# A memory-bound decode kernel: the last 512 columns of one wq row per partition, in place of 384, go to other partitions, spread over five DMA engines instead of three

## The chip, the cores and the metric

One core of a Trainium2 chip runs the kernel. The metric is device time in microseconds (us) of one launch; lower is better. In what follows PE is TensorE (the matrix multiplier), DVE VectorE, ACT ScalarE, and SP the engine whose queue issues the loads. The kernel before takes 138.09 us (median of 6 runs, 137.95 to 138.22).

## The reference

A decode step with four tokens: layer norm, attention over the last 2,048 positions of a cache, output projection, residual, then layer norm and a gated MLP with its residual. Every weight and cache row is read once, 55.6 MB in all.

```python
# shapes: x (4,1,1024); k_cache, v_cache (4,4,8192,128); wq (1024,4096); wo (4096,1024)
#         w1, w3 (1024,3584); w2 (3584,1024); all bf16
def A(x, k_cache, v_cache, wq, wo):        # 32 query heads, 4 kv heads, window W = 2048
    q = (x @ wq).reshape(...)              # <- the change touches how wq is loaded
    p = softmax(q . k[last W] / sqrt(128))
    return (p . v[last W]) @ wo
h   = x + A(layernorm(x), ...)
out = h + (silu(layernorm(h) @ w1) * (layernorm(h) @ w3)) @ w2
```

## The kernel before

All weights and caches flow through one ring (a buffer that is filled and freed in turn) in SBUF, the on-chip memory, by loads of 128 partitions issued from one queue, in the order wq, k, v, wo, w1, w3, w2. Partition p holds the eight wq rows 8p to 8p+7. The last 384 columns of each partition's eighth row do not go to the ring: the tail load stops short of them, and three small loads ("side" loads) put these 128 pieces of 768 B onto 12, 12 and 8 partitions.

```python
CE = 384
SETS = [(0, 3, 5), (60, 3, 5), (120, 2, 1)]      # first row, engines, pieces side by side per partition

def load_side(r0, ne, ns):
    t = ktpool.tile([P, JG * QD * 16], BF16, tag="kT")
    rows = A_wq[r0 * KC : (r0 + ne * 4 * ns) * KC, N_Q - CE : N_Q]
    rows = rows.rearrange("(t i k) n -> k i t n", i=ne, k=KC)[KC - 1]
    nc.sync.dma_start(out=t[: ne * 4, : ns * CE], in_=rows)
    return [t[: ne * 4, k * CE : (k + 1) * CE] for k in range(ns)]

def load_tail(at, src, n, r0, m):
    t = ring[:, at : at + m * n]
    nc.sync.dma_start(out=t[:, : m * n - CE], in_=src[:, r0 * n : (r0 + m) * n - CE])
    return [t[:, k * n : (k + 1) * n] for k in range(m)]

plan = [
    ("wq", load_rows, (0, wq_v, N_Q, 0, 4)),      # 4 rows a partition: 32,768 B each
    ("side", load_side, SETS[0]), ("side", load_side, SETS[1]), ("side", load_side, SETS[2]),
    ("wq", load_tail, (32 * KIB, wq_v, N_Q, 4, 4)),
    # ... k, v, wo, w1, w3 ...
    ("w2", load_rows, (56 * KIB, w2_v, D, 0, 17)),
    ("w2", load_rows, (90 * KIB, w2_v, D, 17, 7)),
    ("w2", load_rows, (104 * KIB, w2_v, D, 24, 3)),
    ("w2", load_rows, (110 * KIB, w2_v, D, 27, 1)),
]
# ...
x_sb = act.tile([B, D], BF16)
nc.scalar.dma_start(out=x_sb[:], in_=x_flat)     # 4 partitions: its packets mark engines 0 to 3
load_next(8)
# ... layer norm; xs / ts_ps / xsT hold the entries of x that belong to the side pieces ...
for kc in range(KC):
    # ... q += xnT[kc] @ wq[kc], the last 384 columns left out at kc == 7 ...
    if kc == RQ - 1:
        for k, np_ in enumerate(sl):             # the side pieces: 11 small matmuls
            nc.tensor.matmul(q_ps[QD * (JG - 1) : QD * (JG - 1) + B, CQ - CE : CQ],
                             lhsT=xsT[:np_, k, :], rhs=loaded["side"][k], start=False, stop=False)
```

Why anyone would do this: a 128-partition load is split over 16 DMA engines, eight partitions each. The side loads run on the lowest-numbered engines alone. The Trainium skill, "DMA: Bandwidth & Descriptors", section "Why a DMA increments its semaphore by 16 and not by 1" ("How many engines (k)"), says that a load runs on the largest k up to 16 that divides the slowest dimension of both sides, and on the lowest-numbered k of the engines. Here these are 12 partitions and 3 blocks of rows, so three engines, and the trace agrees: it has packets of 768 B in three engines' sequences alone, 44, 44 and 40 of them. So the piece takes 6,144 B from every engine and loads three of them with more: it moves work from engine to engine.

Of the kernel before, what the change touches and what calls it, by code (L numbers as in the profile page):

```python
# [14 lines left out]
BF16 = mybir.dt.bfloat16  # L15
# [4 lines left out]
def kernel(  # L20
# [13 lines left out]
    nc = tc.nc  # L34

    B, _, D = A_x.shape
# [5 lines left out]
    KC = D // P  # L42
# [16 lines left out]
    wide = ctx.enter_context(tc.tile_pool(name="wide", bufs=2))  # L59
    const = ctx.enter_context(tc.tile_pool(name="const", bufs=1))  # L60
    act = ctx.enter_context(tc.tile_pool(name="act", bufs=1))
# [46 lines left out]
    N_Q, N_F = Hq * Dh, F  # L108


    CE = 384
    SETS = [(0, 3, 5), (60, 3, 5), (120, 2, 1)]

    def load_side(r0, ne, ns):

# [11 lines that stand above are left out]
    KIB = 512  # L127
    plan = [
        ("wq", load_rows, (0, wq_v, N_Q, 0, 4)),
        ("side", load_side, SETS[0]),  # L130
        ("side", load_side, SETS[1]),
        ("side", load_side, SETS[2]),
        ("wq", load_tail, (32 * KIB, wq_v, N_Q, 4, 4)),
# [16 lines left out]
    def load_next(n=1):  # L150
        for _ in range(n):
            if cursor[0] < len(plan):
                kind, f, args = plan[cursor[0]]
                loaded.setdefault(kind, []).extend(f(*args))
                cursor[0] += 1
# [19 lines left out]
    for c in range(2):  # L175
# [8 lines left out]
        out=xn[:], in0=x_sb[:], scalar1=mv[:, 0:1], scalar2=rstd[:, 0:1],  # L184
# [9 lines left out]

    NS = sum(ns for _, _, ns in SETS)
    ts_ps = psA.tile([P, NS, B], BF16, tag="kt1")
    xs = wide.tile([B, NS, 12], BF16, tag="w4k")
    sl = []
    for r0, ne, ns in SETS:
        v = xn[:, r0 * KC : (r0 + ne * 4 * ns) * KC]  # L200
        v = v.rearrange("b (s l i k) -> b k l i s", s=4, l=ns, i=ne)
        nc.vector.tensor_copy(
            out=xs[:, len(sl) : len(sl) + ns, : ne * 4].rearrange("b l (i s) -> b l i s", s=4),
            in_=v[:, KC - 1, :, :, :],
        )
        for l in range(ns):
            nc.tensor.transpose(
                out=ts_ps[: ne * 4, len(sl), :], in_=xs[:, len(sl), : ne * 4], identity=ident[:B, :B]
            )
            sl.append(ne * 4)  # L210
    xsT = act.tile([12, NS, B], BF16)
    nc.vector.tensor_copy(out=xsT[:, : NS - 1, :], in_=ts_ps[:12, : NS - 1, :])
    nc.vector.tensor_copy(out=xsT[:8, NS - 1 :, :], in_=ts_ps[:8, NS - 1 :, :])


    q_ps = psA.tile([P, CQ], FP32, tag="scores")
# [9 lines left out]
        out=perm[:].rearrange("p (h dq) -> p h dq", dq=JG),  # L226
        in_=ident[:].rearrange("p (dq h) -> p h dq", dq=JG),
# [12 lines left out]
    for j in range(2, JG):  # L240
        nc.vector.tensor_tensor(
            out=same[:, 0, :], in0=same[:, 0, :], in1=ident[:, j * QD : (j + 1) * QD], op=ALU.add
# [6 lines left out]
    for kc in range(KC):  # L249
        wq_t = loaded["wq"][kc]  # L250
        for hf in range(CQ // 512):
            for g in range(JG):
                c0 = g * CQ + hf * 512
                n = min(512, N_Q - CE - c0) if kc == KC - 1 else 512
                nc.tensor.matmul(  # L255
                    q_ps[QD * g : QD * g + B, hf * 512 : hf * 512 + n],
                    lhsT=xnT[:, kc, :],
                    rhs=wq_t[:, c0 : c0 + n],
                    start=(kc == 0),
                    stop=(kc == KC - 1),  # L260
                )
        if kc == RQ - 1:
            load_next()
            for k, np_ in enumerate(sl):
                nc.tensor.matmul(
                    q_ps[QD * (JG - 1) : QD * (JG - 1) + B, CQ - CE : CQ],
                    lhsT=xsT[:np_, k, :],
                    rhs=loaded["side"][k],
                    start=False,
                    stop=False,  # L270
                )
# [4 lines left out]
    for r in range(REP):  # L276
        nc.tensor.transpose(out=qt_ps[:, r, :], in_=q_sb[:, r * Dh : (r + 1) * Dh], identity=ident[:])
    nc.vector.tensor_copy(
        out=qz[:, :, : Hkv * QD].rearrange("p b (g z) -> p b g z", g=Hkv)[:, :, :, :REP],
        in_=qt_ps[:].rearrange("p r (g x) -> p x g r", g=Hkv)[:, :B, :, :],  # L280
# [24 lines left out]
    for u, (b, n) in enumerate(units):  # L305
        k_v = loaded["k"][b]
        kT = ktpool.tile([P, NJ, P], BF16, tag="kT")
        for t in range(NJ // TB):
            kt_ps = psA.tile([P, TB, P], BF16, tag=f"kt{nt % 4}")
            for jj in range(TB):  # L310
                nc.tensor.transpose(  # L311
                    out=kt_ps[:, jj, :], in_=k_v[:, n * NJ + t * TB + jj, :], identity=ident[:]
# [21 lines left out]
        out=Pm[:], in_=scores_ps[:], func=ACT.Exp, bias=nmax[:], scale=1.0, accum_out=rsum[:]  # L334
# [6 lines left out]
    for c in range(NSB):  # L341
# [4 lines left out]
        for g in range(Hkv):  # L346
            if g % 2 == 0:
                nc.vector.tensor_scalar(  # L348
                    out=z[:, :, g, :], in0=pt_ps[:], scalar1=mask[:, g : g + 1], scalar2=None, op0=ALU.mult
# [10 lines left out]
        out=Dm[:], in0=ident[:].rearrange("p (g b r) -> p b g r", g=Hkv, b=B),  # L360
# [11 lines left out]
    for b in range(B):  # L372
        for j in range(JK):
# [5 lines left out]
                stop=(j == JK - 1),  # L379
# [19 lines left out]
    for i in range(IO):  # L399
        for j in range(JG):  # L400
# [5 lines left out]
                stop=(i == IO - 1),  # L406
# [27 lines left out]
        out=hn[:], in0=h1[:], scalar1=tot[:, 0:1], scalar2=rstd2[:, 0:1],  # L434
# [5 lines left out]
        out=hnT[:].rearrange("p k x -> p (k x)"), in_=hn[:].rearrange("q (c k) -> q k c", k=KC)  # L440
# [5 lines left out]
    def gate_up(kind, out_ps):  # L446
# [27 lines left out]
        out=hgT[:].rearrange("p i x -> p (i x)"),  # L474
        in_=hg[:].rearrange("q s c -> q (s c)").rearrange("q (c i) -> q i c", i=IF),
# [3 lines left out]
    for i in range(IF):  # L479
        for j in range(JG):  # L480
# [5 lines left out]
                stop=(i == IF - 1),  # L486
# [36 lines left out]
```

## Time and profile before

| | before |
|---|---|
| time, median of 6 runs | 138.09 us |
| span of the profiled run | 136.2 us |
| TensorE / VectorE / ScalarE busy | 52% / 32% / 23% |
| queue of the loads | 55.58 MB, 95.5% of 16 engines' span |
| last landing of a weight load | 132.80 us |

From the page of the kernel before: busy tenths of the DMA engines in 40 equal slices, then the queues (packets, MB, share of 16 engines' span).

```profile
DMA  5999999999999999999989999999899999999970
## 3 DMA queue, kind: packets, MB, share of 16 engines
q1 hardware_dynamic: 2728, 55.58, 95.5%
q8 instruction: 8, 0.13, 0.3%
q10 hardware_dynamic: 48, 0.02, 0.1%
q14 instruction: 2, 0.02, 0.0%
```

The DMA engines are 80% busy or more from the second slice to the 38th. The chain of waits says the same from the other end; its last pieces (start, length, what; a DMA piece runs from the issue of a load to its landing):

```profile
3.70 19.98 DMA ring<-in_A_wq_dram
...
73.34 1.46 PE OT_ps L374 x48
74.82 24.12 DMA ring<-in_B_w_dram
98.98 2.41 PE g_ps L451 x21
...
101.52 31.28 DMA ring<-in_B_w_dram
...
132.84 0.32 PE y_ps L481 x4
```

At 74.82 us the attention matmuls (OT_ps) have freed room in the ring, w1 is issued and lands 24.1 us later, behind the loads that were issued before it. The last load of w2 is issued at 101.5 us and lands after 31.3 us, at 132.80; PE and the store need little after that. These pieces are time in the queue, not slowness of one load: the engines never run dry. A kernel whose end is set by a stream of loads is bound by whichever of the 16 engines finishes last, because a load has landed only when all its engines have.

**Reading the engines one by one.** The profile's views add the engines up. The trace also has one record for each DMA packet, with start, duration, size and queue, but not its engine. On one engine a packet starts 3 to 4 ns before the one ahead of it is recorded as ended, and every engine must go through the same known sequence of sizes (eight packets a load, then a 4 B completion). Matching ends to starts under that rule gives 16 sequences with no packet left over. Engines that did the same work then agree within about 10 ns over 119 us, which is the check on the method. Its weak point: two engines whose packets end within a few ns of each other can be exchanged. Below, times in the stream count from the start of the first packet of the loads (1.73 us into the span), and the "finish" of an engine is the start of its last completion record.

What the sequences of the kernel before hold, apart from the same loads for all:

| engines | extra work | finish |
|---|---|---|
| 0, 1, 2 | 44, 44, 40 side pieces of 768 B, one every 33 ns | 130.62, 130.74 (order unknown), 130.49 |
| 3 | one 8 KB packet of queue 14 in between | 130.08 |
| eight others | one 16 KB packet of queue 8 ("instruction") each: "hit" below | 130.24 to 130.76 |
| four others | none | 128.83 to 129.35 |

An instruction packet takes 0.88 to 0.96 us, and the data packet after it takes 0.4 to 0.5 us longer than its like: 1.42 us in all for that engine. The first three rows are nearly level, and the four unhit engines are done 1.4 us early or more.

### The profile page before, as it was taken

What the parts mean: (1) busy time and instruction counts of PE and PEld (TensorE: products, weight loads), DVE (VectorE), ACT (ScalarE), POOL (GpSimd) and SP (SyncE); (2) the same over time, 40 slices, a digit from 0 to 9 for tenths busy, and PEclk for the clock granted to TensorE, in tenths of its full rate; (3) what the DMA queues carried; (4) which work ended last, traced back from release to release, by engine and by line L of the source; (5) the groups of instructions that cost most, each with busy time, mean ns of one, the idle gap of its engine ahead of it and who ended that gap; (6) DMA issues with size and microseconds to landing.
All of it is one profiled execution on the core that took longest, in us unless ns stands there. A gap on an engine that the chain in (4) does not pass through costs nothing.

```text
span 136.2 us, 2356 instructions
## 1 busy us (share of the span) xinstructions
PE 71.4 (52%) x1057; PEld 44.1 (32%) x1057; DVE 43.2 (32%) x78; ACT 31.0 (23%) x36; POOL 1.7 (1%) x8
## 2 busy tenths in 40 slices
PE   0202980969898989602275858810095440900960
PEld 0200220266565656200054747610042210300830
DVE  6810000054343425454972030260000794080000
ACT  3000000037373737445666000000004200000001
POOL 5000000000000000000000000000000000000000
PEclk9999999999999999955555595995559555555586
DMA  5999999999999999999989999999899999999970
GB/s 156 463 464 406 407 432 411 424 438 424 428 438 414 443 428 424 438 532 462 443 385 424 448 424 392 489 392 455 362 413 443 430 455 442 419 419 407 420 280 5
DMA packets 2786, 55.75 MB, mean 409 GB/s; under 512 B 308, under 2 KB 468, under 8 KB 728
## 3 DMA queue, kind: packets, MB, share of 16 engines
q1 hardware_dynamic: 2728, 55.58, 95.5%
q8 instruction: 8, 0.13, 0.3%
q10 hardware_dynamic: 48, 0.02, 0.1%
q14 instruction: 2, 0.02, 0.0%
HBM read 55.59 MB, written 0.01 MB: 408 GB/s over the span
## 4 chain that ended last, share of the span: by engine, by line
DMA 55%; PE 21%; ACT 13%; DVE 5%; SPq 2%; issue 1%; ACTq 0%
DMA ring<-in_B_w_dram 41%; DMA ring<-in_A_wq_dram 15%; PE kt_ps L311 9%; ACT kT L317 6%; PE scores_ps L296 5%; ACT z L352 3%; PE q_ps L255 3%; PE g_ps L451 2%; SPq L119 2%; DVE rmax L328 2%; ACT Pm L333 2%; PE OT_ps L374 2%; DVE pT L342 1%; DVE z L348 1%; ACT L333 1%
## 5 line engine op out<-in xcount | busy, mean ns | idle before, releaser
L317 ACT COPY kT<-kt_ps 128x1024 bf16<-128x1024 bf16 x16 | 15.8, 1013 | 12.0 <-PE kt_ps L311 12.0
L311 PE MATMUL kt_ps<-ident,ring 128*128 128x128 bf16 x256 | 16.5, 219 | 0.0
L311 PEld LDWEIGHTS <-ring 128*128 128x128 bf16 x256 | 14.4, 98 | 5.0 <-issue 4.9
L315 DVE COPY kT<-kt_ps 128x1024 bf16<-128x1024 bf16 x16 | 11.1, 692 | 15.2 <-PE kt_ps L311 15.2
L451 PEld LDWEIGHTS <-hnT 128*32 128x32 bf16 x128 | 5.2, 134 | 23.7 <-issue 21.0
L255 PE MATMUL q_ps<-ring,xnT 128*4 128x512 bf16 x64 | 7.2, 621 | 10.5 <-DMA ring<-in_A_wq_dram 10.5
L296 PE MATMUL scores_ps<-kT,qz 128*32 128x512 bf16 x64 | 9.9, 610 | 3.1 <-ACT kT L317 3.1
L451 PE MATMUL u_ps<-ring,hnT 128*32 128x448 bf16 x64 | 6.4, 576 | 8.7 <-DMA ring<-in_B_w_dram 8.7
L374 PE MATMUL OT_ps<-z,ring 128*128 128x32 bf16 x256 | 7.5, 186 | 5.7 <-ACT z L352 5.0
L451 PE MATMUL g_ps<-ring,hnT 128*32 128x448 bf16 x64 | 5.1, 496 | 9.5 <-DMA ring<-in_B_w_dram 9.5
L481 PE MATMUL y_ps<-ring,hgT 128*32 128x256 bf16 x112 | 5.6, 362 | 8.5 <-DMA ring<-in_B_w_dram 8.4
L374 PEld LDWEIGHTS <-ring 128*128 128x128 bf16 x256 | 7.3, 103 | 6.4 <-issue 6.4
L481 PEld LDWEIGHTS <-hgT 128*32 128x32 bf16 x112 | 4.3, 126 | 10.4 <-issue 6.2
L273 DVE TENSOR_SCALAR q_sb<-q_ps 128x512 bf16<-128x512 f32 x1 | 0.7, 692 | 19.9 <-PE q_ps L255 19.9
L255 PEld LDWEIGHTS <-xnT 128*4 128x4 bf16 x64 | 2.0, 116 | 14.6 <-issue 14.5
L491 ACT CAST res<-y_ps 128x256 bf16<-128x256 f32 x1 | 0.4, 372 | 26.8 <-PE y_ps L481 26.8
L352 ACT ACTIVATE z<-pt_ps,mask 128x512 bf16<-128x512 f32 x8 | 5.3, 688 | 3.5 <-DVE z L348 3.5
L401 PE MATMUL y_ps<-ring,o 128*32 128x256 bf16 x128 | 5.4, 344 | 1.3 <-DMA ring<-in_A_wo_dram 1.3
L274 ACT ACTIVATE q_sb<-q_ps 128x512 bf16<-128x512 f32 x1 | 0.6, 597 | 23.8 <-DVE q_sb L273 23.8
L344 PE MATMUL pt_ps<-pT,perm 128*128 128x512 bf16 x4 | 2.4, 609 | 6.8 <-DVE pT L342 6.8
L348 DVE TENSOR_SCALAR z<-pt_ps,mask 128x512 bf16<-128x512 f32 x8 | 5.5, 740 | 1.2 <-ACT z L352 0.8
L465 DVE RECIPROCAL eg<-eg 128x896 f32<-128x896 f32 x1 | 5.8, 5753 | 0.0
(80 smaller groups left out, 50.9 us busy)
## 6 DMA issues: line engine op xcount, KB each, us to landing
ring<-in_A_k_cache_dram SPq DMA_DIRECT2D x4, 2048.0 KB, 25.4
ring<-in_A_v_cache_dram SPq DMA_DIRECT2D x4, 2048.0 KB, 38.8
ring<-in_B_w_dram SPq DMA_DIRECT2D x1, 7168.0 KB
ring<-in_B_w_dram SPq DMA_DIRECT2D x2, 3584.0 KB, 27.9
ring<-in_B_w_dram SPq DMA_DIRECT2D x1, 4352.0 KB
ring<-in_A_wq_dram SPq DMA_DIRECT2D x1, 4096.0 KB, 12.1
ring<-in_A_wq_dram SPq DMA_DIRECT2D x1, 4000.0 KB, 20.0
ring<-in_B_w_dram SPq DMA_DIRECT2D x1, 1792.0 KB
```

The lines of the kernel that those rows point to most:

```text
L255: nc.tensor.matmul(q_ps[QD * g : QD * g + B, hf * 512 : hf * 512 + n], lhsT=xnT[:, kc, :], rhs=wq_t[:, c0 : c0 + n], start=(kc == 0), stop ...
L296: nc.tensor.matmul(scores_ps[QD * g : QD * (g + 1), n * 512 : (n + 1) * 512], lhsT=qz_v[:, z0 : z0 + QD], rhs=kT_v[:, g, :, :], start=(b = ...
L311: nc.tensor.transpose(out=kt_ps[:, jj, :], in_=k_v[:, n * NJ + t * TB + jj, :], identity=ident[:])
L315: nc.vector.tensor_copy(out=kT[:, t * TB : (t + 1) * TB, :], in_=kt_ps[:])
L317: nc.scalar.copy(out=kT[:, t * TB : (t + 1) * TB, :], in_=kt_ps[:])
L348: nc.vector.tensor_scalar(out=z[:, :, g, :], in0=pt_ps[:], scalar1=mask[:, g : g + 1], scalar2=None, op0=ALU.mult)
L352: nc.scalar.mul(out=z[:, :, g, :], in_=pt_ps[:], mul=mask[:, g : g + 1])
L374: nc.tensor.matmul(OT_ps[:, b, :], lhsT=loaded["v"][b][:, j, :], rhs=PTz[j // NJ][:, (j % NJ) * B + b, :, :], start=(j == 0), stop=(j == J ...
L401: nc.tensor.matmul(y_ps[QD * j : QD * (j + 1), :], lhsT=o4[:, i, :, :].rearrange("p b s -> p (b s)"), rhs=loaded["wo"][i][:, j * CG : (j + ...
L451: nc.tensor.matmul(out_ps[QD * j : QD * (j + 1), hf, :HF], lhsT=hnT[:, k, :], rhs=loaded[kind][k][:, c0 : c0 + HF], start=(k == 0), stop=( ...
L465: nc.vector.reciprocal(out=eg[:], in_=eg[:])
L481: nc.tensor.matmul(y2_ps[QD * j : QD * (j + 1), :], lhsT=hgT[:, i, :], rhs=loaded["w2"][i][:, j * CG : (j + 1) * CG], start=False, stop=(i ...
```

## The change

Its intent, as far as the code shows it: take more from every engine (512 columns, 8 x 1,024 B instead of 8 x 768 B) and, so that engines 0 to 2 do not get more than they have, let engines 3 and 4 take a part. 80 rows go to 20 partitions (20 and 5: five engines, 16 rows each), 48 rows in two loads to 12 partitions (three engines, 16 more rows each). The wq columns that are loaded this way now are a whole 512-column block of the matmul, so one of the 64 matmuls falls away.

```diff
@@ -108,8 +108,8 @@
     N_Q, N_F = Hq * Dh, F
 
 
-    CE = 384
-    SETS = [(0, 3, 5), (60, 3, 5), (120, 2, 1)]
+    CE = 512
+    SETS = [(0, 5, 4), (80, 3, 2), (104, 3, 2)]
 
     def load_side(r0, ne, ns):
 
@@ -194,7 +194,7 @@
 
     NS = sum(ns for _, _, ns in SETS)
     ts_ps = psA.tile([P, NS, B], BF16, tag="kt1")
-    xs = wide.tile([B, NS, 12], BF16, tag="w4k")
+    xs = wide.tile([B, NS, 20], BF16, tag="w4k")
     sl = []
     for r0, ne, ns in SETS:
         v = xn[:, r0 * KC : (r0 + ne * 4 * ns) * KC]
@@ -208,9 +208,11 @@
                 out=ts_ps[: ne * 4, len(sl), :], in_=xs[:, len(sl), : ne * 4], identity=ident[:B, :B]
             )
             sl.append(ne * 4)
-    xsT = act.tile([12, NS, B], BF16)
-    nc.vector.tensor_copy(out=xsT[:, : NS - 1, :], in_=ts_ps[:12, : NS - 1, :])
-    nc.vector.tensor_copy(out=xsT[:8, NS - 1 :, :], in_=ts_ps[:8, NS - 1 :, :])
+    xsT = act.tile([20, NS, B], BF16)
+    k0 = 0
+    for _, ne, ns in SETS:
+        nc.vector.tensor_copy(out=xsT[: ne * 4, k0 : k0 + ns, :], in_=ts_ps[: ne * 4, k0 : k0 + ns, :])
+        k0 += ns
 
 
     q_ps = psA.tile([P, CQ], FP32, tag="scores")
@@ -252,12 +254,14 @@
             for g in range(JG):
                 c0 = g * CQ + hf * 512
                 n = min(512, N_Q - CE - c0) if kc == KC - 1 else 512
+                if n <= 0:
+                    continue
                 nc.tensor.matmul(
                     q_ps[QD * g : QD * g + B, hf * 512 : hf * 512 + n],
                     lhsT=xnT[:, kc, :],
                     rhs=wq_t[:, c0 : c0 + n],
                     start=(kc == 0),
-                    stop=(kc == KC - 1),
+                    stop=(kc == KC - 1 or (kc == KC - 2 and c0 + 512 == N_Q)),
                 )
         if kc == RQ - 1:
             load_next()
```

## The prediction

> **What bounds the kernel.** The profile of before spans 136.2 us. Its DMA row is at 8 or 9 in all slices but the first and the last two; the queue table gives queue 1 95.5% of 16 engines' span. The chain of waits ends in weight loads (24.1 and 31.3 us of waiting for ring<-in_B_w, last landing at 132.80 us); after it come 0.32 us of PE, 0.37 us of ACT and the store. PE is 52% busy, inside the stream. The DMA engine that finishes last sets the time.
>
> I rebuilt the 16 engines' packet sequences from the DMA packet records. They run without a gap, except that
> - engines 0 to 2 carry the side rows: 44, 44 and 40 packets of 768 B, one per 33 ns, 1.33 to 1.47 us;
> - eight engines are each hit once by a 16 KB instruction packet (queue 8; 0.88 to 0.96 us, and the next data packet is 0.4 to 0.5 us longer): 1.42 us. The Trainium skill, "Runtime: NRT & Kernel Launch", "Instruction fetch mechanics", has instructions refilled in 16 KiB blocks of 256; the trace agrees, with 8 such packets for 2,122 PE records;
> - one engine has an 8 KB packet (queue 14, next to the Exp table load), 0.84 us. The x loads mark engines 0 to 3, and by them this is engine 3.
>
> Finishes, us after the first weight packet: four engines with none of these 128.83 to 129.35; engine 3 130.08; engines 0 to 2 130.62, 130.74, 130.49 (the first two may be swapped); the eight hit ones 130.24 to 130.76. That is already level.
>
> **The change.** "DMA: Bandwidth & Descriptors", "How many engines (k)", has a DMA split over the largest k up to 16 that divides the slowest dimensions of both sides: 12 and 3 gave 3 engines, as the packets show; 20 and 5 should give 5. Per engine (a 1,024 B packet estimated at 43 ns, between 33 ns for 768 B and 80 ns for 2,048 B; 32,768 B take 1.213 us):
> - all: 8 x 256 B less in the tail load, -0.076 us;
> - engines 0, 1: 44 x 33 becomes 32 x 43 ns, with the tail -0.17 us; engine 2: -0.04;
> - engines 3, 4: 16 new packets, +0.69 - 0.08 = +0.61 us.
>
> PE loses 14 instructions (3 side matmuls, 3 small transposes, one 512-column matmul, with weight loads); the wq tail may land 0.17 us earlier. All of it lies inside the stream, off the critical path.
>
> **Sum.** Hit engines: 130.76 -> 130.69. Engine 3: 130.08 -> 130.70. Engines 0, 1: at most 130.57. Engine 4: the order of first packets suggests that it is unhit, so about 129.7. The last finish moves by -0.06 us: I predict 138.06 us, 137.80 to 138.40. Faster by over 2%: 0.5%; within 2%: 99%; slower by over 2%: 0.5%.
>
> **What would show it.** 128 packets of 1,024 B near 45 ns in place of those of 768 B, 80 of them on five engines; 11 side completions instead of 8; 31,744 B packets near 1.175 us; eight instruction packets on eight engines; the engine with the 8 KB packet has 16 side rows and finishes near 130.7; the last landing near 132.7 us, and all after it as before.
>
> **What would make it wrong.** Engine 4 may be a hit one: then it ends at 130.8 to 131.4, and the kernel is 0.1 to 0.6 us slower. The last instruction packet comes in the last 3 us: 14 instructions fewer may shift it past its engine's last data, which helps that engine alone. The engines start 0.4 us apart and may do so in another order; the runs of before spread over 0.18 us, more than the effect.

## The result

The change runs at 138.01 us (median of 6 runs, 137.80 to 138.18) against 138.09 us (137.95 to 138.22). The ratio is 0.9994 with a 95% interval of 0.9981 to 1.0007: the same.

The page of the changed kernel, the same lines as above:

```profile
DMA  5999999999999999999979999989899999989970
## 3 DMA queue, kind: packets, MB, share of 16 engines
q1 hardware_dynamic: 2731, 55.58, 95.6%
q8 instruction: 8, 0.13, 0.3%
q10 hardware_dynamic: 48, 0.02, 0.1%
q14 instruction: 2, 0.02, 0.0%
```

Three packets more on queue 1 are the three completions more (5 + 3 + 3 engines instead of 3 + 3 + 2). The bytes are the same, and so is the number of instruction packets. The chain of waits after:

```profile
3.80 19.77 DMA ring<-in_A_wq_dram
...
74.49 1.46 PE OT_ps L378 x48
75.97 22.91 DMA ring<-in_B_w_dram
98.92 2.41 PE g_ps L455 x17
101.46 31.31 DMA ring<-in_B_w_dram
```

The attention matmuls freed the room for w1 1.15 us later than in the profile of before (75.97 against 74.82), and yet w1 landed no later: PE starts on it at 98.92 against 98.98. The queue in front of it was long enough. What happens on PE before that does not matter here.

The loads of wq, from the list of issues (KB each, us to landing), before and then after:

```profile
ring<-in_A_wq_dram SPq DMA_DIRECT2D x1, 4096.0 KB, 12.1
ring<-in_A_wq_dram SPq DMA_DIRECT2D x1, 4000.0 KB, 20.0
t<-in_A_wq_dram SPq DMA_DIRECT2D x2, 45.0 KB
t<-in_A_wq_dram SPq DMA_DIRECT2D x1, 6.0 KB
```

```profile
ring<-in_A_wq_dram SPq DMA_DIRECT2D x1, 4096.0 KB, 12.1
ring<-in_A_wq_dram SPq DMA_DIRECT2D x1, 3968.0 KB, 19.8
t<-in_A_wq_dram SPq DMA_DIRECT2D x1, 80.0 KB
t<-in_A_wq_dram SPq DMA_DIRECT2D x2, 24.0 KB
```

The 128 packets are of 1,024 B now and take 46 ns each (those of 768 B took 36). Engine by engine, the clearest measure is the time from an engine's first completion to its last, which leaves out when the engine started. It repeats within 10 ns or so in the second traces of both kernels (runs 9 and 10 below):

| role | before | after | difference | forecast |
|---|---|---|---|---|
| engines 0, 1 | 120.04 | 119.87 | -0.17 | -0.17 |
| engine 2 | 119.90 | 119.87 | -0.03 | -0.04 |
| engine 3 | 119.45 | 120.02 | +0.57 | +0.61 |
| engine 4 | 118.62 (as the unhit) | 119.18 | +0.57 | +0.61 |
| hit engines | 120.04 | 119.96 | -0.08 | -0.076 |
| unhit engines | 118.62 | 118.54 | -0.08 | -0.076 |

(Two hit sequences of the first trace after read 120.03 and 120.10, most likely where two sequences were exchanged, and one reads 119.73, because its instruction packet came among the last small packets.) Last to finish is engine 3 now, at 130.72; hit engines follow at 130.34 to 130.67, engines 0 to 2 at 130.39 to 130.63; engine 4 ends at 129.58. So the finish moved from 130.76 to 130.72.

### The profile page after: what moved, and what is told of

The parts are those of the page before. It is cut to its first block, busy times and chain, and to the rows that moved or that the text cites. A ratio compares the mean times of both kernels' runs of the same rounds, so it can differ in the third digit from the quotient of the medians.

```text
span 136.1 us, 2343 instructions
## 1 busy us (share of the span) xinstructions
PE 73.8 (54%) x1050; PEld 45.0 (33%) x1050; DVE 43.4 (32%) x79; ACT 31.1 (23%) x36; POOL 1.7 (1%) x8
## 4 chain that ended last, share of the span: by engine, by line
DMA 54%; PE 24%; ACT 11%; DVE 5%; SPq 2%; issue 1%; ACTq 0%
DMA ring<-in_B_w_dram 40%; DMA ring<-in_A_wq_dram 15%; PE kt_ps L315 10%; ACT kT L321 5%; PE scores_ps L300 5%; ACT z L356 3%; PE q_ps L259 3%; SPq L119 2%; PE g_ps L455 2%; DVE rmax L332 2%; ACT Pm L337 2%; PE OT_ps L378 2%; DVE pT L346 1%; DVE z L352 1%; ACT L337 1%
## 5 line engine op out<-in xcount | busy, mean ns | idle before, releaser
L315 PE MATMUL kt_ps<-ident,ring 128*128 128x128 bf16 x256 | 17.8, 230 | 0.0
L315 PEld LDWEIGHTS <-ring 128*128 128x128 bf16 x256 | 15.8, 104 | 4.9 <-issue 4.9
L378 PEld LDWEIGHTS <-ring 128*128 128x128 bf16 x256 | 7.4, 105 | 9.8 <-issue 9.7
```

The source lines that it names most:

```text
L315: nc.tensor.transpose(out=kt_ps[:, jj, :], in_=k_v[:, n * NJ + t * TB + jj, :], identity=ident[:])
L378: nc.tensor.matmul(OT_ps[:, b, :], lhsT=loaded["v"][b][:, j, :], rhs=PTz[j // NJ][:, (j % NJ) * B + b, :, :], start=(j == 0), stop=(j == J ...
```

## The experiments

Three theories stood at first. **A**: the engine that finishes last sets the time, and each engine's time is the sum of its own packets. **B**: the engines share one limit of bytes, so moving bytes between them does nothing; the flat result would fit this as well. **C**: the path over the landing of wq sets the time. Ten kernels were run, all correct, all with five timed rounds, on three chips (runs 1 to 4, 5 to 8, 9 and 10); each ratio is to the kernel before in the same rounds. Below, "slower" means only that the interval lies above 1. Edits are against the changed kernel; those that alter `SETS` also make the number of side loads and the tiles' 20 partitions follow it (not shown). The results together, with the last finish in the stream and the tail from the end of that completion to the end of the span, from the one profiled run of each:

| run | last finish | tail | span | median us | ratio to before [95% interval] |
|---|---|---|---|---|---|
| before | 130.76 | 3.66 | 136.2 | 138.09 | |
| after | 130.72 | 3.66 | 136.1 | 138.01 | 0.9994 [0.9981, 1.0007] |
| 1 no side rows | 130.91 | 3.83 | 136.5 | 138.36 | 1.0032 [1.0018, 1.0045] |
| 2 two engines | 132.30 | 3.81 | 137.9 | 139.32 | 1.0099 [1.0085, 1.0113] |
| 3 eight engines | 130.93 | 4.05 | 136.7 | 138.58 | 1.0045 [1.0033, 1.0057] |
| 4 width only | 130.96 | 3.86 | 136.6 | 138.43 | 1.0034 [1.0022, 1.0047] |
| 5 more on 3 and 4 | 130.91 | 3.64 | 136.3 | 138.20 | 1.0016 [1.0003, 1.0028] |
| 6 spread only | 130.73 | 3.62 | 136.1 | 138.01 | 1.0000 [0.9987, 1.0012] |
| 7 six engines | 130.83 | 3.70 | 136.3 | 138.07 | 1.0010 [0.9998, 1.0023] |
| 8 more PE instructions | 131.89 | 3.85 | 137.5 | 139.24 | 1.0089 [1.0075, 1.0102] |
| 9 after again | 130.79 | 3.66 | 136.2 | 138.00 | 0.9996 [0.9984, 1.0009] |
| 10 before again | 130.69 | 3.64 | 136.1 | 137.95 | 0.9994 [0.9981, 1.0008] |

### 1: no side rows

```diff
-    CE = 512
-    SETS = [(0, 5, 4), (80, 3, 2), (104, 3, 2)]
+    CE = 0
+    SETS = []          # and no xs, ts_ps, xsT, no side matmuls
```

> No side rows at all: every engine carries the same 8 full wq rows. Theory A (the engine that finishes last sets the time): the instruction-hit engines get 0.23 us longer than before (8 x 768 B given back) and finish last at about 130.99 us after the first weight packet, against 130.76 before: ratio to before 1.0017, about 138.3 us. Engines 0 to 2 then finish near 129.6, engine 3 near 130.3. Theory B (one common limit of bytes for all engines): the bytes are the same, ratio 1.000. Theory C (the path over the wq landing sets the time): the last wq row lands about 1.3 us earlier, so faster by about 1 us, ratio near 0.993.

Measured: slower, 1.0032. Seven hit engines end last, from 130.55 to 130.91; the eighth instruction packet came at 129.40, too late to hold up its engine's data. The eight engines with neither a hit in time nor the 8 KB packet end at 129.23 to 129.51, the one with the 8 KB packet at 130.24. Theory C falls by the chain of waits of this run:

```profile
1.17 21.29 DMA ring<-in_A_wq_dram
22.49 3.22 PE q_ps L235 x32
...
71.73 1.46 PE OT_ps L354 x48
73.21 25.79 DMA ring<-in_B_w_dram
99.04 2.41 PE g_ps L431 x16
101.58 31.33 DMA ring<-in_B_w_dram
```

wq was there 1.2 us earlier (q starts at 22.49 against 23.72), w1 was issued 1.6 us earlier (73.21 against 74.82), and it took 1.67 us longer to land. All of the head start was spent in the queue: PE starts on w1 at 99.04 against 98.98. The size was not as forecast: the last finish came 0.14 us later than in the first trace of before, not 0.23, and the time grew by 0.34 us. The tail took the rest of it: it was 0.17 us longer (see the end of this section).

### 2: all side rows on two engines

```diff
-    SETS = [(0, 5, 4), (80, 3, 2), (104, 3, 2)]
+    SETS = [(0, 2, 4), (32, 2, 4), (64, 2, 4), (96, 2, 4)]
```

> All 128 side rows of 1,024 B on engines 0 and 1, 64 each. Theory A: these two finish at 129.57 - 0.30 + 64 x 0.043 = 132.0, 1.24 us after the last of before: ratio 1.009, about 139.3 us. Theory B: 1.000. Theory C: wq lands 1.2 us later, about 1.009 as well; this run tells A from B, the one without side rows tells A from C.

Measured: 1.0099, against 1.009 for theory A and 1.000 for theory B. Theory B falls: the same bytes over the same 16 engines take 1.3 us longer when two engines carry the side rows. These two end at 132.14 and 132.30, 0.1 to 0.3 us over the forecast. Their packet records account for that: the 1,024 B packets came 45 and 47 ns apart here, against 43 in the changed kernel and in run 4, which over 64 packets is 0.15 and 0.26 us; why they did stays open. Other engines stood idle for 0.2 to 1.3 us near 78 us in the stream, which no other trace shows. That fits loads being issued late because an earlier load waited for the two late engines, but only the idle time itself was seen. It does not explain the loss: the two engines that finish last have no gap there.

### 3: eight engines, 16 rows each

```diff
-    SETS = [(0, 5, 4), (80, 3, 2), (104, 3, 2)]
+    SETS = [(0, 8, 4)]
```

> 128 side rows of 1,024 B on engines 0 to 7, 16 each: the trace shows directly which instruction-hit engines are among the first eight, since only engines 0 to 7 carry 1,024 B packets. My guess from the order of first packets is that engines 4, 5, 6 and 15 are not hit and 7 to 14 are. Then one engine with 16 rows and a hit finishes at 131.0 to 131.35, 0.25 to 0.6 us after the last of before: ratio 1.002 to 1.004. If the hits are on 8 to 15 alone: last at 130.7 as after the change, ratio 0.9995. If several of 4 to 7 are hit: ratio near 1.004. Theory B: 1.000. Theory C: wq lands 0.7 us earlier, ratio 0.995.

Eight engines carry packets of 1,024 B, as 32 partitions and 8 blocks should give. Two of them are hit as well, and these two finish last, at 130.92 and 130.93; from first completion to last they take 120.60 us, 1.42 us more than those with 16 rows and no hit (119.18). So the guess of one hit engine among the first eight was wrong; it is two. The forecast of 131.0 to 131.35 was a little high, because both of these engines happened to start early (first completions at 10.32, in a range from 10.28 to 10.83). With theory A the order is right: an engine with both burdens is the last. Most of the measured loss, however, is tail: 0.39 us of it (4.05 against 3.66), where the last finish moved by 0.16. (The eighth instruction packet came at 129.19, after its engine's last data, as in run 1.)

### 4: the width alone

```diff
-    SETS = [(0, 5, 4), (80, 3, 2), (104, 3, 2)]
+    SETS = [(0, 3, 4), (48, 3, 4), (96, 3, 2), (120, 2, 1)]     # 44, 44, 40 rows, as before
```

> Half of the change: 512 columns, but with the old spread (44, 44 and 40 rows on engines 0 to 2). Theory A: engines 0 and 1 finish at 129.57 - 0.30 + 44 x 0.043 = 131.15, 0.39 us after the last of before: ratio 1.0028, about 138.5 us. Theory B: 1.000.

Measured: 1.0034. Engines 0 to 2 are the last three, at 130.96, 130.86 and 130.81; the hit engines are at 130.65 at the latest. The forecast of 131.15 was 0.2 us high, which the start again explains in part (first completions at 10.47 and 10.57, against 10.58 and 10.69 before); from first completion to last these engines take 120.39 us, 0.34 us more than before. Of the 0.41 us that the time grew, 0.20 is the last finish and 0.20 the tail. Half of the change alone is a loss.

### 5: eight rows more on engines 3 and 4

```diff
-    SETS = [(0, 5, 4), (80, 3, 2), (104, 3, 2)]
+    SETS = [(0, 5, 4), (80, 5, 2), (120, 2, 1)]
```

> Eight rows of 1,024 B more on engines 3 and 4 (24 instead of 16), 28 on engines 0 and 1, 24 on engine 2. Engine 3 (the one with the 8 KB table packet) finished last after the change, at 130.72. Theory A: it now finishes at 130.72 + 8 x 0.043 = 131.06, all others at 130.7 or earlier, engine 4 near 129.9: last finish 0.30 us after that of before, ratio 1.002 plus up to 0.001 of the end of the program (the last drain grew by 0.15 to 0.4 us in the four kernels tried so far). Theory B (common limit): 1.000.

Measured: 1.0016, the interval just above 1. The engine with the 8 KB packet is the last, at 130.91, and 0.29 us behind the next one (130.62). From first completion to last it takes 120.37 us against 120.02: 43 ns a row, as estimated. So the change stops where it has to: engine 3 cannot take more.

### 6: the spread alone

```diff
-    CE = 512
+    CE = 384
```

> The other half of the change: 384 columns as before, with the new spread (32 rows on engines 0 to 2, 16 on 3 and 4). Theory A: the instruction-hit engines keep their bytes, so the last finish stays at 130.76 or so (engines 0 to 2 near 130.3, engine 3 near 130.6): ratio 1.000 to 1.001. So the new spread gains nothing alone, and the width alone lost; only the two together keep level.

Measured: 1.0000. Hit engines are last, at 130.73, with 120.04 us from first completion to last as before; engines 0 to 2 end at 130.29 to 130.33. Neither half gains: the width alone overloads engines 0 to 2, the spread alone relieves engines that were not the last by much.

### 7: six engines, engine 3 relieved

```diff
-    SETS = [(0, 5, 4), (80, 3, 2), (104, 3, 2)]
+    SETS = [(0, 6, 3), (72, 3, 4), (120, 2, 1)]     # 32, 32, 28, 12, 12, 12 rows
```

> Rows of 1,024 B: 32 on engines 0 and 1, 28 on 2, 12 on 3, 4 and 5. Engine 3 comes off the end (130.72 - 0.17 = 130.55), so by theory A the last is an instruction-hit engine at 130.4 to 130.7: ratio 0.999 to 1.001, no gain that can be told from the noise. The trace tells whether engine 5 is hit: two of 5, 6 and 7 are, by the run with eight engines; if the hits go in order of time over neighbouring engines, they start at 6, and engine 5 is unhit and finishes near 129.5.

This was meant as the best split that such loads allow. It is no better: 1.0010. Of the three engines with 12 rows, one has the 8 KB packet, one is unhit, and one is hit; the hit one is last, at 130.83 (120.43 us from first completion to last: 0.47 for its rows and 1.42 for the hit over an engine with neither). So engine 4 or 5 is hit here, 5 if engine 4 stays unhit as in the other runs, and my guess that the hits begin at engine 6 was wrong. Which engines are hit beyond that stays open, and whether they are the same ones in every kernel.

### 8: 260 more PE instructions

```diff
+    dm_ps = psA.tile([P, KC, B], BF16, tag="kt2")
+    for _ in range(130):
+        nc.tensor.transpose(out=dm_ps[:, 0, :], in_=xn_v[:, 0, :], identity=ident[:B, :B])
```

> The changed kernel with 130 small transposes more on PE (260 instructions) early, while PE waits for wq. They should cost one 16 KB instruction packet more, nine in place of eight. If these packets go over neighbouring engines in turn, the ninth goes to an engine that had none and finished near 129.2: that one ends near 130.65, and the time stays as after the change (ratio 0.999 to 1.001). If it falls on engines 0 to 3, or on one that already has one, that engine ends at 132.0 to 132.1 and the ratio is near 1.009. If the packets have nothing to do with the number of PE instructions, there are eight.

The queue table of this run:

```profile
## 3 DMA queue, kind: packets, MB, share of 16 engines
q1 hardware_dynamic: 2731, 55.58, 94.6%
q8 instruction: 9, 0.15, 0.4%
```

There are nine instruction packets instead of eight, for 2,368 PE records; the other traces have eight for 2,078 to 2,140. The first (11.73 us into the stream) and the ninth (129.14) are in one engine's sequence, which finishes at 131.89, 1.3 us after the last of the other hit engines and 1.0 us after engine 3 (130.91); seven others have one packet each. So in this run the packets go round eight engines and the ninth comes back to the first: not the main guess, an engine that had none, but the second one, an engine that already has one. The time rises by 1.3 us (1.0089) although the 130 transposes cost PE nothing that lasted. They ran from 6.25 to 14.2 us and held up the first half of q by 1.3 us (14.15 against 12.86 after the change), but PE then waited 4.0 us for the rest of wq and started on it at 23.56 (23.61 after the change):

```profile
99.11 2.06 PE g_ps L459 x21
101.18 32.24 DMA ring<-in_B_w_dram
133.46 1.04 PE y_ps L489 x15
```

The cost came through the loads. The chain shows the last load but one (three rows of w2), which lands at 133.42 us (101.18 + 32.24), where before PE could start on it at 132.22. By the trace's semaphore records the last weight load lands at 134.03 instead of 132.80. This is the strongest support for theory A, since no load was touched: a packet of 16 KB, 0.03% of the bytes, on one engine that had no slack, makes the kernel 0.9% slower.

### 9 and 10: both kernels again

Unaltered copies.

> The changed kernel once more, unaltered: does the last finish repeat? With the service times that the traces so far agree on (118.55 us from an engine's first completion to its last for an engine with no side rows and no hit; 1.42 more for a hit; 0.84 for the table packet; 0.64 for 16 rows, 1.33 for 32), engine 3 and the hit engines should again end within 0.3 us of each other, the last between 130.6 and 131.0; ratio 0.998 to 1.001.

> The kernel before as a kernel of its own against itself: what the measurement calls the same. Ratio 0.9985 to 1.0015; last finish between 130.6 and 131.0, set by where the engines start, since the service times (118.62 us, 1.42 more for a hit) do not change. If last finishes of the same kernel differ by 0.1 us or more between two traces, the change's 0.04 us in the first pair of traces is not to be called a gain.

Measured: 0.9996 for the change and 0.9994 for the kernel before against itself. The last finishes are 130.79 (engine 3 again) and 130.69 (a hit engine). The first pair of traces had the change 0.04 us ahead, this pair has it 0.10 us behind. The times from first completion to last repeated; the starts did not: first completions lie between 10.21 and 10.78 us, dealt to the engines in another way in each trace. The engines' first packets begin up to 0.9 us apart in these two traces and take anything from 1.21 to 2.08 us, where the later ones of that size take 1.21.

**The tail.** In runs 1 to 4, 7 and 8 the end of the program is 0.04 to 0.4 us longer. The instruction records after the output has landed show SP going through one 28 ns wait before its drain in before and after, but through two to four, 60 to 70 ns apart, in runs 1 to 4; in run 3 the last drain on ACT comes 0.33 us later as well. Run 8 has one such wait, like before; there 0.11 us of the 0.19 lies between the landing of the last load and the end of PE's last matmul (0.47 against 0.36 us). The list of waits has a trace of it: in run 4 SP came to the wait for the output before the others.

```profile
SPq L518 <- DMA out_dram<-res: 2.5, 1, 2.5
```

```profile
SPq L521 <- DMA out_dram<-res: 9.3, 1, 9.3
```

The first line is of before, the second of run 4 (us in total, times, longest). The order of these closing waits varies from kernel to kernel; what decides it was not looked into. It must be taken off before a few tenths of a microsecond are read as the effect of a load. With it, the last finish and the tail of run 1 add up to 0.14 + 0.17 = 0.31 us over the first trace of before, where the time rose by 0.34. (The tail is the span less the last finish, so such sums must come out; what the split shows is how little of the loss in runs 1, 3 and 4, 0.14 to 0.20 us, is the loads'.)

## Why the prediction was right

- **What bounds the kernel**: shown. The engine that finishes last sets the time: runs 2 and 8 make one or two engines late and pay 1.3 us; run 1 brings wq and the attention forward by over 1 us and gains nothing. Runs 1, 3, 4 and 5 agree in which engine is last, but their last finishes moved by 0.14 to 0.20 us only.
- **Cost per engine**: the forecast sums were within 0.04 us for every role (table in the result). The one term that was off is the 16 rows on engines 3 and 4: +0.57 in place of +0.61. (A slip without effect: the matmul that fell away had 128 columns, by the trace of before, not 512.)
- **Engine 3 becomes the last**: as forecast, at 130.72 and 130.79 in two traces against 130.70. Run 5 shows that it has nothing left to give.
- **Engine 4 is unhit**: as forecast (129.58 against 129.7), though the order of first packets, from which I took it, misled me about engines 5 to 7 in runs 3 and 7.
- **The instruction packets stay eight, one to an engine, and late ones help only their own engine**: as forecast; the last came at 128.65 instead of 128.35 us, and its engine took 0.23 us less than the other hit ones. In runs 1 and 3 it came after its engine's last data, as the prediction had thought possible.
- **Size**: 138.06 was forecast and 138.01 measured. A forecast of no change at all would have done as well, so the time alone tests nothing here; the table of the engines does. The forecast gain of 0.06 us itself is not confirmed: the kernel before, measured against itself, gives 0.9994, and the last finishes of the two pairs of traces differ in sign. What is shown is that the change is worth less than the lottery of the engines' starts, about 0.1 us. The prediction's link of the 8 KB packet to the Exp table load rested on its time alone; no run tests it.

Why so large a rearrangement is worth so little: engines 0 to 2 and the hit engines were level to begin with, engine 3 some 0.5 us ahead of them; the change moves engines 0 and 1 by -0.17 us, engine 3 by +0.57 and the hit ones by -0.08, so that all are level. The hit engines can be relieved only through the width, 0.08 us for 128 columns, and each widening has to be carried by the few low-numbered engines with slack. An estimate of what is left: the 16 finishes after the change average 130.20, the last is 130.72, so a perfect levelling would gain 0.5 us, 0.4%. Run 7, the nearest that loads of this kind came to it, did not gain.

## What to carry to other kernels

When a kernel's end is set by a stream of loads, read the DMA engines one by one, not as a mean: 95% busy hid 1.4 us of slack on some engines and none on others. Work out what each engine gets before moving bytes between them, because what one engine ends late the kernel ends late (1.3 us in runs 2 and 8), while levelling engines that are already nearly level gained nothing here. Before calling a few tenths of a microsecond a gain, measure the old kernel against itself and take the start and the end of the program apart from the stream.

## What the Trainium skill lacked or had wrong

- "Runtime: NRT & Kernel Launch", section "Instruction fetch mechanics", calls the cost of crossing a 16 KiB block of instructions "mostly hidden". In this kernel, bound by its loads, it is not: each block that came before an engine's last small packets delayed that engine's data by 1.42 us, and a ninth block on an engine that already had one made the kernel 1.3 us slower (run 8). The page does not say on which DMA engines the blocks are fetched; in run 8 nine blocks went round eight of the 16.
- "DMA: Bandwidth & Descriptors", section "Specifications", gives about 27 GiB/s an engine. Here 32,768 B took 1.213 us, which is 27.0 GB/s, 7% less than 27 GiB/s. Its section "Where 436 GB/s comes from" says without a condition that the HBM side binds loads at about 358 GB/s; with one core running, the DMA engines moved 409 GB/s over the whole span. The page's own note under "Measured" has it right: about 358 GB/s is each core's part when both cores of an HBM stream, and one core alone reached 425 GB/s for 16 MB (loads issued from GpSimd).
- The same page's rule for the number of engines was right in each case that the traces show: 12 and 3, 20 and 5, 8 and 2, 32 and 8, 24 and 6 gave 3, 5, 2, 8 and 6 engines.
- No page tells that the first packets of a stream begin and take unequally (in the traces of before and after they begin up to 0.47 us apart and take 1.59 to 2.08 us for 32,768 B, later 1.21), so that the engines run 0.4 to 0.7 us out of step at their first completions, in another order in each trace, and keep that difference.
- No page tells that the end of a program differs between kernels whose last instructions are alike: from the last completion record of the weight loads to the end of the span 3.62 to 4.05 us passed. ("Runtime: NRT & Kernel Launch" lists the stages of a postamble with one time for each.)
